# Chunked attention into a top-2 expert layer: x turned for the logits by transposing transfers instead of TensorE, and the turned P copied by ScalarE

## The chip, the cores and the metric

The kernel runs on one core of a Trainium2 chip. The metric is the device time of one execution in microseconds, the median of several runs. The engines are TensorE (PE, with PEld for its weight loads), VectorE (DVE), ScalarE (ACT), GpSimd (POOL) and SyncE (SP); SPq and POOLq are the queues in which SP and POOL issue transfers (DMAs). Each engine works through its own instructions in order; semaphores make them wait for each other. SBUF is the memory on the core with 128 partitions, PSUM the one that TensorE writes.

## What is computed

An attention over chunks, whose output is the token matrix x of a mixture-of-experts layer:

```python
batch, n_heads, seq, head_dim = (4, 8, 768, 64)
chunk, left_ctx, right_ctx = (32, 16, 8)          # and 8 memory keys and values
for c in range(seq // chunk):
    k_full = np.concatenate([mem_k, k[:, :, l_start:r_end]], axis=2)
    v_full = np.concatenate([mem_v, v[:, :, l_start:r_end]], axis=2)
    scores = scale * np.matmul(q_c, k_full.transpose(0, 1, 3, 2))
    a = softmax(scores)
    out[:, :, c_start:c_end] = np.matmul(a, v_full)
x = out.transpose(0, 2, 1, 3).reshape(3072, 512)

logits = x @ w_gate
noisy_logits = logits + np.log1p(np.exp(x @ w_noise)) * noise
top2 = np.argpartition(-noisy_logits, 2, axis=1)[:, :2]     # 8 experts
# softmax over the two; then for each expert e and its tokens:
out[mask] += top2_w * (np.maximum(x[mask] @ w1[e], 0.0) @ w2[e])
```

## The kernel before, in words

The program has two stages. The attention stage makes x and the routing; the expert stage gathers the tokens of each pair of experts and runs the two expert matmuls. Here only the first matters.

The attention is worked in 16 pairs, n = 0 to 15, four to a batch (HP = 4). A loop over i runs the pairs as a pipeline: iteration i does the max and the exponential of pair i, the PV matmuls of pair i - 1, the scores of pair i + 1 and the turning of q and k of pair i + 2. For a pair n these steps exist, each named in the code:

- `qkT_pe` turns q and k on PE into PSUM; ACT copies them to SBUF (qT at L268, and kd in two halves at L276).
- `scores_pe` writes the scores ps_s (there is one such buffer, so the scores of pair i + 1 wait until the subtraction of pair i has read the last ones).
- `max_dve` (mx, L313) and `sub_dve` (sd, L318) are DVE's; ACT makes P = exp(sd) at L320.
- `PT_pe` turns P on PE into p_p (L327); `PT_dve` copies it to PT in SBUF (L332).
- `PV_pe` multiplies with the memory values (L341) and the values (L345) into ps_o.
- `mult_dve` divides (rec at L357, xrow at L358): xrow is the buffer of x of one batch, three of them in turn.
- `xT_pe` turns 6 blocks of 128x128 of xrow on PE into p_x (L369), and ACT copies them into xt (L371). xt has five buffers, one per pair.

After four pairs, `begin_route(b)` runs in iteration i = 4b + 6: `logits_pe(b)` multiplies the four xt tiles of batch b with the router weights wgn (24 matmuls at L380), and the steps s1 to s8 of `route(b)` are spread over the next iterations as "early" and "late" steps. Step s4 makes the gates (L463 to L466, into xrow) and issues the write of the batch's x rows to memory (`write_rows`, x_rows at L548), from which the expert stage gathers by index. After the loop comes the routing of batch 3.

The order of instructions on each engine is that of the code, written out by hand; nothing reorders it. SP's queue carries, besides the x_rows writes, the loads of the memory values (mv_nat), of the router weights (wgn_f, two loads, at i = 3) and of the noise (nz_all, four loads: one with wgn_f, one at the routing of batch 0, two at that of batch 1). The loads of q, k, v and the expert weights are issued by POOL. PSUM tiles of the kinds p_t, p_p, p_x and the routing's share three buffers (psT).

Of the kernel before, what the change touches and what calls it, by code (L numbers as in the profile page):

```python
# [13 lines left out]
BF16 = mybir.dt.bfloat16  # L14
# [10 lines left out]
def kernel(  # L25
# [14 lines left out]
    nc = tc.nc  # L40
    B, H, S, D = q.shape
# [11 lines left out]
    HP = H // 2  # L53
# [45 lines left out]
    def body():  # L99
        actx = ExitStack()  # L100
        ap_ = actx.enter_context(tc.tile_pool(name="ap", bufs=2))
# [14 lines left out]
        def new_group(g):  # L116
            qg = ap_.tile([128, 2 * GP, SJ * D], BF16, name="qg", bufs=3)
            kg = ap_.tile([128, 2 * GP, SJ * D], BF16, name="kg", bufs=3)
            groups[g] = (qg, kg, vbufs[turn_of[g]])
# [8 lines left out]
        def load_v(g):  # L128
            vg = groups[g][2]
            for hd in range(2 * GP):  # L130
                p0, gh = QW * hd, 2 * GP * g + hd

                def piece(c, n, j=0, nj=WP):
                    nc.gpsimd.dma_start(  # L134
                        out=vg[p0 + j:p0 + j + nj, c:c + n, hd, :, :].rearrange("p c e d -> p c (e d)"),
                        in_=bass.AP(v.tensor, v.offset + (gh * S + c * chunk + 2 * j - left_ctx) * D, [[2 * D, nj], [chunk * D, n], [1, 2 * D]]))

                first, last = gh == 0, gh == B * H - 1
                if first:
                    piece(0, 1, left_ctx // 2, WP - left_ctx // 2)  # L140
                if last:
                    piece(ncnk - 1, 1, 0, WP - right_ctx // 2)
                piece(int(first), ncnk - first - last)

        def zero_k(x):
            for hh in range(2):
                nc.vector.memset(kbufs[x][64 * hh:64 * hh + 64, 1 - hh, :], 0.0)

        def zero_v(x, j, eng=None):
            (eng or nc.vector).memset(vbufs[x][:, 6 * j:6 * j + 6], 0.0)  # L150
# [12 lines left out]
        for hd in range(2 * GP):  # L163
            nc.sync.dma_start(
                out=mv_nat[QW * hd + WP:QW * hd + QW].rearrange("p g e d -> p g (e d)"),
                in_=bass.AP(mem_v.tensor, mem_v.offset + hd * n_mem * D, [[2 * D, n_mem // 2], [2 * GP * n_mem * D, NG], [1, 2 * D]]))
# [88 lines left out]
        st = [dict() for _ in range(NPAIR)]  # L255
        xrows = {}

        def qkT_pe(n):
            g, i = divmod(n, GP)
            qg, kg, _ = groups[g]  # L260
            for nm, src in (("qT", qg), ("kT", kg)):
                p_t = psT.tile([128, SJ, 128], BF16, name="p_t", tag="tr")
                for j in range(SJ):
                    for hh in range(2):
                        nc.tensor.transpose(out=p_t[64 * hh:64 * hh + 64, j, :], in_=src[:, 2 * i + hh, j * D:(j + 1) * D], identity=identb)  # L265
                if nm == "qT":
                    st[n][nm] = ap_.tile([128, S], BF16, name=nm, bufs=4)
                    nc.scalar.copy(st[n][nm].rearrange("d (p j) -> d p j", j=SJ), p_t.rearrange("d j p -> d p j"))  # L268
                else:
                    st[n]["p_k"] = p_t  # L270
# [7 lines left out]
        UB = BT // 2  # L278
# [32 lines left out]
        def max_dve(n):  # L311
            mx = ap_.tile([128, 2, BT], F32, name="mx")
            nc.vector.tensor_reduce(out=mx, in_=st[n]["ps"], axis=AX, op=Alu.max)  # L313
            st[n]["mx"] = mx

        def sub_dve(n):
            sd = ap_.tile([128, 2, BT, CTX], F32, name="sd")
            nc.vector.tensor_tensor(out=sd, in0=st[n]["ps"], in1=bc4(st[n]["mx"], CTX), op=Alu.subtract)  # L318
            P = ap_.tile([128, 2 * UB, 4, QW], BF16, name="P")
            nc.scalar.activation(out=P.rearrange("p x h c -> p h x c"), in_=sd.rearrange("p x (h u) (e c) -> p (x h) (u e) c", h=2, e=2), func=Act.Exp, scale=scale)  # L320
            st[n]["P"] = P

        def PT_pe(n):
            P = st[n]["P"]
            p_p = psT.tile([128, 2 * UB, 128], BF16, name="p_p", tag="tr")
            for x in range(2 * UB):
                nc.tensor.transpose(out=p_p[:, x, :], in_=P[:, x, :, :], identity=identb)  # L327
            st[n]["p_p"] = p_p

        def PT_dve(n):  # L330
            PT = ap_.tile([128, 2 * UB, 128], BF16, name="PT")
            nc.vector.tensor_copy(PT, st[n]["p_p"])  # L332
            st[n]["PT"] = PT

        def PV_pe(n):
# [27 lines left out]
        def xT_pe(n):  # L363
            b, r = divmod(n, HP)
            y, half = divmod(r, 2)
            p_x = psT.tile([128, UB, 2, 128], BF16, name="p_x", tag="tr")
            for u in range(UB):
                for s in range(2):
                    nc.tensor.transpose(out=p_x[:, u, s, :], in_=xrows[b][:, UB * half + u, 128 * y + 64 * s:128 * y + 64 * s + 64].bitcast(BF16), identity=identb)  # L369
            xt = ap_.tile([128, UB, 2, 128], BF16, name="xt", bufs=5)  # L370
            nc.scalar.copy(xt, p_x)  # L371
            st[n]["xt"] = xt
# [180 lines left out]
        def begin_route(b):  # L553
            logits_pe(b)
            begin, *rest = route(b)
            begin()
            while pending:
                early_steps()
                late_steps()
            pending.extend(rest)  # L560
            for x in ((1,), (2, 3))[b] if b < 2 else ():
                load_noise(x)

        def early_steps():
            if pending:
                for fn in pending[0][0]:
                    fn()
# [19 lines left out]
        def ahead(i):  # L587
            return [i + 2] if i < NEAR else [n for n in (i + 2, i + 3) if n < NPAIR and (i == NEAR or n > i + 2)]

        NEAR = 5  # L590
        for i in range(NPAIR):
            if i >= 1:
                PT_pe(i - 1)
            max_dve(i)
            for n in ahead(i):
                qkT_pe(n)
            fresh = i >= 3 and (i - 3) % HP == HP - 1
            if fresh:
                begin_route((i - 3) // HP)
            early_steps()  # L600
            if i >= 1:
                PT_dve(i - 1)
            sub_dve(i)
            if i == 0:
                zero_v(1, 1)
                load_v(1)
                new_group(3)
                load_qk(3)
            if i == 1:
                zero_k(3)  # L610
            for n in ahead(i):
                kT_act(n)
            if i >= 1:
                PV_pe(i - 1)
            if i + 1 < NPAIR:
                scores_pe(i + 1)
            if i < NPAIR - 1:
                late_steps()
            if i in (2, 3, 4):
                zero_v(2, i - 2)  # L620
            if i >= 1:
                mult_dve(i - 1)
                if i - 1 == NPAIR - 2:
                    write_rows(B, B - 1, 0, UB, 0, XC)
            if i >= 2:
                xT_pe(i - 2)
            if i == 2:
                load_v(2)
                memory_values(2, NG)
            for n in ahead(i):  # L630
                g = n // GP + 3
                if n % GP == 1 and g < NG:
                    new_group(g)
                    load_qk(g)
            if i == 3:
                zero_v(2, 3, nc.gpsimd)
                ramps()
                load_router()
            if i == 4:
                load_v(3)  # L640
            if i == 5:
                constants()
            if i >= 4 and i % GP == 0 and i // GP + 2 < NG:
                load_v(i // GP + 2)
            if i == GP * (NG - 3) + 1:
                load_w1(0)
                load_w2(0)
                load_w1(1)
        n = NPAIR - 1
# [227 lines left out]
        for e in range(E):  # L877
# [38 lines left out]
            if e == E - 1:  # L916
# [3 lines left out]
                    out=out_part[NB], out_offset=bass.IndirectOffsetOnAxis(ap=s_si[:, 0:1], axis=0),  # L920
                    in_=spart[:, 0, :], in_offset=None, bounds_check=N - 1, oob_is_err=False)
# [6 lines left out]
    with tc.manual_schedule():  # L928
        kept = body()
# [3 lines left out]
    with tc.For_i(SPILL, end, 128) as i:  # L933
# [7 lines left out]
        for t in range(NP):  # L941
# [11 lines left out]
            out=xl, out_offset=None, in_=xd, in_offset=bass.IndirectOffsetOnAxis(ap=gi[:, 0:1], axis=0),  # L953
# [4 lines left out]
        xt = ld.tile([128, KP, CAP], BF16, name="xtl", bufs=1)  # L958
# [5 lines left out]
        with tc.For_i(0, E, 1) as e:  # L964
# [17 lines left out]
            out=out, out_offset=bass.IndirectOffsetOnAxis(ap=si[:, 0:1], axis=0),  # L982
            in_=o, in_offset=None, bounds_check=N - 1, oob_is_err=False)
# [30 lines left out]
```

## Time and profile before

| | |
|---|---|
| median of 3 runs | 334.02 us (332.93 to 334.89) |
| the profiled execution, its own time | 335.33 us |
| its span in the trace | 333.7 us |
| PE busy over the span | 288.1 us (86%) |
| DVE, ACT, POOL busy | 169.9, 133.4, 138.6 us |
| first max of the attention loop | 14.74 us |
| first gather of the expert stage | 114.24 us |
| mean granted TensorE clock | 0.957 of full speed |

The profile is of one execution. A row of a timeline or of the chain of waits begins with the start and the length in us; L with a number is the line of the code; `out<-in` are the tiles. A group of instructions has its count (x16), the busy time in us and the mean of one in ns, and behind the bar the idle time before them and what ended it. The chain of waits is followed back from the last instruction: at each step to what released it. "issue" is time in which an engine waited for nothing that the profile shows.

### The profile page before, as it was taken

The page shows a single profiled execution, that of the slowest core. Times are in us where ns is not written, and L with a number is a line of the kernel's source. Part 1 is how long each engine was busy: PE and PEld are TensorE (multiplying, and loading weights), DVE is VectorE, ACT ScalarE, POOL GpSimd, SP SyncE. Part 2 cuts the span into 40 slices and gives each one's busy share as a digit, 9 for nine tenths or more (in the row PEclk, how much of TensorE's full clock was granted, in tenths as well). Part 3 has the DMA queues.
Part 4 walks back from the last instruction along what each step waited for, and adds up shares of the span by engine and source line. Part 5 has one row for each costly group of instructions (what it writes and reads, how often), then busy time and mean ns, then how long its engine had stood idle before and what let it go on. Part 6 is the DMA issues. An engine that isn't in the chain of part 4 may idle for free.

```text
span 333.7 us, 7301 instructions
## 1 busy us (share of the span) xinstructions
PE 288.1 (86%) x3019; PEld 173.5 (52%) x3019; DVE 169.9 (51%) x343; ACT 133.4 (40%) x235; POOL 138.6 (42%) x181
## 2 busy tenths in 40 slices
PE   1697887977776377999999999999999999999990
PEld 0575675755654256554754754544544544544540
DVE  7789859849958775222322323424342433434451
ACT  7877788757433033533333332332303303202200
POOL 7877868538023472781008007007152042042152
PEclk9999999979989559999999999999999999999997
DMA  7999999999997136699407905914959624521031
GB/s 99 179 163 176 184 163 163 210 143 101 214 225 216 23 88 93 128 156 238 87 0 125 221 4 110 223 28 105 207 147 166 117 111 70 86 109 60 1 140 71
DMA packets 58763, 42.99 MB, mean 129 GB/s; under 512 B 32449, under 2 KB 52033, under 8 KB 58728
## 3 DMA queue, kind: packets, MB, share of 16 engines
q0 software_dynamic: 49808, 38.71, 77.0%
q1 hardware_dynamic: 8632, 3.74, 5.6%
q8 instruction: 24, 0.39, 0.5%
q10 hardware_dynamic: 288, 0.07, 0.1%
q14 instruction: 11, 0.09, 0.1%
HBM read 61.23 MB, written 10.66 MB: 215 GB/s over the span
## 4 chain that ended last, share of the span: by engine, by line
PE 43%; issue 24%; DVE 13%; ACT 8%; POOL 7%; DMA 3%; POOLq 0%; DVEq 0%; ACTq 0%
PE ps_h L769 16%; PE ps_y L780 14%; POOL out_dram L788 4%; ACT kd L276 3%; PE ps_o L345 3%; DMA out_dram<-acc,sidx 2%; PE ps_o L341 2%; DVE mx L313 2%; DVE xrow L358 2%; DVE sd L318 2%; DVE vg L150 2%; PE p_t L705 2%; ACT xt L371 1%; ACT P L320 1%; PE p_t L265 1%
## 5 line engine op out<-in xcount | busy, mean ns | idle before, releaser
L769 PE MATMUL ps_h<-xTb,w1t 128*128 128x512 bf16 (+5 forms) x640 | 101.4, 320 | 1.5 <-DVE xTb L706 1.5
L780 PE MATMUL ps_y<-w2t,ht 128*128 128x512 bf16 x448 | 101.4, 379 | 0.0
L769 PEld LDWEIGHTS <-w1t 128*128 128x128 bf16 x640 | 58.6, 99 | 43.9 <-DVE xTb L706 1.1
L788 POOL DMA_INDIRECT out_dram<-acc,sidx x28 | 28.1, 1004 | 126.4 <-DVE acc L787 124.1
L756 DVE TENSOR_SCALAR ht<-ps_h 128x512 bf16<-128x512 f32 (+3 forms) x68 | 38.1, 560 | 68.1 <-PE ps_h L769 63.1
L780 PEld LDWEIGHTS <-ht 128*128 128x128 bf16 x448 | 42.9, 98 | 46.7
L754 ACT ACTIVATE ht<-ps_h 128x384 bf16<-128x384 f32 (+2 forms) x76 | 38.9, 511 | 70.4 <-PE ps_h L769 66.3
L784 ACT ACTIVATE acc<-ps_y,meta 128x512 f32<-128x512 f32 x28 | 19.2, 687 | 62.6 <-PE ps_y L780 45.4
L787 DVE SCALAR_TENSOR_TENSOR acc<-ps_y,meta,acc 128x512 f32<-128x512 f32 x28 | 21.0, 750 | 34.5 <-PE ps_y L780 34.5
L696 POOL DMA_INDIRECT xl<-x_rows,gidx x28 | 30.0, 1071 | 16.8 <-PE ps_h L769 6.6
L134 POOL DMA_DIRECT2D vg<-in_v_dram x34 | 25.5, 756 | 11.4 <-DMA kg<-in_k_dram 3.7
L706 DVE COPY xTb<-p_t 128x512 bf16<-128x512 bf16 x28 | 11.6, 422 | 28.6 <-PE p_t L705 28.4
L276 ACT COPY kd<-p_t 64x768 bf16<-64x768 bf16 x32 | 25.2, 786 | 1.0 <-PE p_t L265 0.8
L265 PE MATMUL p_t<-identb,qg 128*64 128x128 bf16 x192 | 10.3, 245 | 12.0 <-DMA qg<-in_q_dram 6.6
L371 ACT COPY xt<-p_x 128x768 bf16<-128x768 bf16 x16 | 12.8, 798 | 12.0 <-PE p_x L369 11.9
L341 PE MATMUL ps_o<-memv,PT 128*128 128x260 bf16 x96 | 15.0, 296 | 2.2 <-DVE PT L332 2.0
L320 ACT ACTIVATE P<-sd 128x768 bf16<-128x768 f32 x16 | 13.5, 845 | 8.1 <-DVE sd L318 8.1
L268 ACT COPY qT<-p_t 128x768 bf16<-128x768 bf16 x16 | 12.8, 800 | 8.9 <-PE p_t L265 8.8
L358 DVE TENSOR_TENSOR xrow<-ps_o,rec 128x768 bf16<-128x768 f32 x16 | 15.3, 958 | 0.6
L313 DVE TENSOR_REDUCE mx<-ps_s 128x12 f32<-128x768 f32 x16 | 15.1, 942 | 0.5 <-PE ps_s L300 0.5
L318 DVE TENSOR_TENSOR sd<-ps_s,mx 128x768 f32<-128x768 f32 x16 | 15.2, 949 | 0.0
L345 PE MATMUL ps_o<-vg,PT 128*32 128x256 bf16 x384 | 14.9, 293 | 0.0
(150 smaller groups left out, 287.5 us busy)
## 6 DMA issues: line engine op xcount, KB each, us to landing
w1t<-in_moe_w_dram POOLq DMA_DIRECT2D x8, 1024.0 KB, 11.4
w2t<-in_moe_w_dram POOLq DMA_DIRECT2D x8, 1024.0 KB, 10.1
vg<-in_v_dram POOLq DMA_DIRECT2D x30, 168.0 KB, 10.2
qg<-in_q_dram POOLq DMA_DIRECT2D x7, 384.0 KB, 9.9
kg<-in_k_dram POOLq DMA_DIRECT2D x7, 384.0 KB, 11.3
x_rows<-xrow SPq DMA_DIRECT2D x3, 792.0 KB
x_rows<-xrow SPq DMA_DIRECT2D x2, 384.0 KB
xl<-x_rows,gidx POOLq DMA_INDIRECT x28, 6.5
```

Of the source, the lines that this page charges most:

```text
L134: nc.gpsimd.dma_start(out=vg[p0 + j:p0 + j + nj, c:c + n, hd, :, :].rearrange("p c e d -> p c (e d)"), in_=bass.AP(v.tensor, v.offset + (g ...
L276: nc.scalar.copy(st[n]["kT"][hs, hh, :].rearrange("d (p j) -> d p j", j=SJ), st[n]["p_k"][hs].rearrange("d j p -> d p j"))
L313: nc.vector.tensor_reduce(out=mx, in_=st[n]["ps"], axis=AX, op=Alu.max)
L318: nc.vector.tensor_tensor(out=sd, in0=st[n]["ps"], in1=bc4(st[n]["mx"], CTX), op=Alu.subtract)
L345: nc.tensor.matmul(out=po[32 * r:32 * r + 32, u, :MD], lhsT=PT[:, 2 * u + e, 32 * r:32 * r + 32], rhs=vg[:, CB * half + x, :, e, :], start ...
L358: nc.vector.tensor_tensor(out=xr.rearrange("p u (h d) -> p u h d", d=D), in0=po[:, :, :MD].rearrange("p u (h d) -> p u h d", d=D), in1=rec ...
L696: nc.gpsimd.indirect_dma_start(out=xl, out_offset=None, in_=xd, in_offset=bass.IndirectOffsetOnAxis(ap=idx[:, p:p + 1], axis=0), bounds_ch ...
L754: nc.scalar.activation(out=dst, in_=src, func=Act.Relu)
L756: nc.vector.tensor_scalar(out=dst, in0=src, scalar1=0.0, scalar2=None, op0=Alu.max)
L769: nc.tensor.matmul(out=ps_h[:, o:o + w], lhsT=w1t[:, kp, f * 128:(f + 1) * 128], rhs=rhs(kp), start=(kp == 0 and i == 0), stop=(kp == KP - ...
L780: nc.tensor.matmul(out=ps_y, lhsT=ht[:, f, j * CAP:(j + 1) * CAP], rhs=w2t[:, f, :], start=(f == 0), stop=(f == FB - 1))
L788: nc.gpsimd.indirect_dma_start(out=out_part[p], out_offset=bass.IndirectOffsetOnAxis(ap=sidx[:, p:p + 1], axis=0), in_=a, in_offset=None, ...
```

## The change

For the batches 0 to 2 (pairs 0 to 11) the six blocks of a pair's x are no longer turned on PE and copied by ACT: SP issues six transposing transfers of 128x128 bf16 each (32 KB), from xrow straight into xt. That is 72 transfers, and 72 PE transposes and 12 ACT copies fewer. Batch 3 is turned as before. For the same twelve pairs the copy of the turned P (PT) is made by ACT and not by DVE, and it stands in the code right behind PE's turning of P, ahead of the turning of q and k, instead of behind the early steps.

```diff
         def PT_dve(n):
             PT = ap_.tile([128, 2 * UB, 128], BF16, name="PT")
-            nc.vector.tensor_copy(PT, st[n]["p_p"])
+            (nc.scalar.copy if n < HP * (B - 1) else nc.vector.tensor_copy)(PT, st[n]["p_p"])
             st[n]["PT"] = PT
...
         def xT_pe(n):
             b, r = divmod(n, HP)
             y, half = divmod(r, 2)
+            if b < B - 1:
+                xt = ap_.tile([128, UB, 2, 128], BF16, name="xt", bufs=5)
+                for u in range(UB):
+                    for s in range(2):
+                        nc.sync.dma_start_transpose(out=xt[:, u, s, :], in_=xrows[b][:, UB * half + u, 128 * y + 64 * s:128 * y + 64 * s + 64].bitcast(BF16))
+                st[n]["xt"] = xt
+                return
             p_x = psT.tile([128, UB, 2, 128], BF16, name="p_x", tag="tr")
...
         for i in range(NPAIR):
             if i >= 1:
                 PT_pe(i - 1)
+                if i - 1 < HP * (B - 1):
+                    PT_dve(i - 1)
             max_dve(i)
...
             early_steps()
-            if i >= 1:
+            if i - 1 >= HP * (B - 1):
                 PT_dve(i - 1)
             sub_dve(i)
```

SP's queue up to the end of the attention stage, before:

```order
L164 DMA mv_nat<-in_mem_v_dram 4x8x128 x4
L209 DMA wgn_f<-in_moe_w_gate_dram 128x4x8
L209 DMA wgn_f<-in_moe_w_noise_dram 128x4x8
L215 DMA nz_all<-in_moe_noise_dram 128x6x8 x2
L548 DMA x_rows<-xrow 128x6x264
L215 DMA nz_all<-in_moe_noise_dram 128x6x8 x2
L548 DMA x_rows<-xrow 128x6x264
```

The same queue after the change, up to the same place:

```order
L164 DMA mv_nat<-in_mem_v_dram 4x8x128 x4
L370 DMA_TRANSPOSE xt<-xrow 128x128 x12
L209 DMA wgn_f<-in_moe_w_gate_dram 128x4x8
L209 DMA wgn_f<-in_moe_w_noise_dram 128x4x8
L215 DMA nz_all<-in_moe_noise_dram 128x6x8
L370 DMA_TRANSPOSE xt<-xrow 128x128 x12
L215 DMA nz_all<-in_moe_noise_dram 128x6x8
L370 DMA_TRANSPOSE xt<-xrow 128x128 x12
L555 DMA x_rows<-xrow 128x6x264
L370 DMA_TRANSPOSE xt<-xrow 128x128 x12
L215 DMA nz_all<-in_moe_noise_dram 128x6x8 x2
L370 DMA_TRANSPOSE xt<-xrow 128x128 x12
```

Twelve transposes are those of two pairs. Those of pairs 0 and 1 now stand ahead of the router weights; those of pairs 6 and 7 stand behind the x_rows write of batch 0; behind the last row shown come the x_rows write of batch 1 and then the twelve of pairs 10 and 11.

ACT around the first routing (iterations 5 and 6) as a piece of the difference; the routing's lines have moved by seven (L395 is now L402):

```order
 L276 COPY kd_88<-p_t 64x768 x2
 L276 COPY kd_85<-p_t 64x768 x2
-L371 COPY xt<-p_x 128x768
+L332 COPY PT<-p_p 128x768
 L268 COPY qT<-p_t 128x768
-L395 ACTIVATE ns<-ps_l 128x48
-L396 ACTIVATE ns<-ns 128x48
-L399 COPY lg<-ps_l 128x48
+L402 ACTIVATE ns<-ps_l 128x48
+L403 ACTIVATE ns<-ns 128x48
+L406 COPY lg<-ps_l 128x48
 L320 ACTIVATE P<-sd 128x4x6x32
```

The PT copy of pair 5 stands where the xt copy of pair 3 stood, between kd and qT.

## The prediction, made before the change was run

> **What bounds the kernel now.** I read four views in this order: the page, the chain of waits from 14 us to 115 us, the timelines of VectorE (DVE) and of SyncE's queue (SPq), and the DMA view. From about 130 us on, the expert matmuls keep TensorE (PE) busy and the change touches nothing there. What it touches is the attention stage, whose end passes straight on. These are rows of the chain (start in us, length in us, what):
>
> ```profile
> 24.60 0.32 issue
> ...
> 47.27 0.74 PE ps_l L380 x24
> ...
> 56.68 0.32 issue
> ...
> 62.68 0.47 DVE PT L332
> ...
> 70.01 0.74 PE ps_l L380 x24
> ...
> 74.06 0.44 PE p_x L369 x6
> ...
> 89.62 0.36 PE p_x L369 x6
> 90.01 0.81 ACT xt L371
> 90.86 0.74 PE ps_l L380 x24
> ...
> 105.39 0.41 PE ps_l L380 x10
> ```
>
> The logits matmuls (L380) of batches 0 to 2 start at 47.27, 70.01 and 90.86 us, and the last ten of batch 3 at 105.39; all four groups lie on the chain, which leads from the last of them over the routing to the first gather and the first expert matmul. So a logits group that starts late pushes everything behind it, one for one.
>
> Between them the pairs run every 4 to 6 us, and no engine bounds all of them: the chain changes between DVE, ScalarE (ACT) and PE. The other pieces quoted are those where the edited steps show. "issue" of 0.32 us stands there four times between the max (mx) and the subtraction (sd) of a pair; the first is at 24.60 and the last at 56.68. It is a busy DVE, as its own timeline shows: the copy of the turned P (L332) runs in that gap.
>
> ```profile
> 22.72 0.96 DVE L358 TENSOR_TENSOR xrow<-ps_o,rec 128x768 bf16<-128x768 f32 x1
> 23.59 0.95 DVE L313 TENSOR_REDUCE mx<-ps_s 128x12 f32<-128x768 f32 x1
> 24.46 0.55 DVE L332 COPY PT<-p_p 128x768 bf16<-128x768 bf16 x1
> ```
>
> **What is removed and swapped.** The groups by line, with count, busy us and mean ns:
>
> ```profile
> L332 DVE COPY PT<-p_p 128x768 bf16<-128x768 bf16 x16 | 8.8, 550 | 0.8 <-PE p_p L327 0.6
> L371 ACT COPY xt<-p_x 128x768 bf16<-128x768 bf16 x16 | 12.8, 798 | 12.0 <-PE p_x L369 11.9
> L268 ACT COPY qT<-p_t 128x768 bf16<-128x768 bf16 x16 | 12.8, 800 | 8.9 <-PE p_t L265 8.8
> ```
>
> Twelve of the 16 copies of PT leave DVE: 12 x 0.55 = 6.6 us, which is the upper bound of what DVE can give back. On the chain they appear as four pieces of 0.32 us and one of 0.47 us, 1.75 us together. On ACT, twelve xt copies of 0.798 us go and twelve PT copies of the same shape come; a PSUM copy of that shape into another tile (qT) takes 0.800 us, so ACT's load is unchanged: 0 us. The PT copy now stands ahead of the qT copy instead of xt, in the place xt had, so nothing on ACT is later; its cover is that exchange, and without it (ACT holding PT back behind the two kd copies) it would cost up to 0.80 us a pair. On PE, 72 transposes go; the chain holds 0.44 + 0.36 us of them, and the xt copy ahead of the third logits is 0.81 us: 1.6 us. **The gain is 1.75 + 1.6 = 3.4 us**, between 0 (if each freed piece uncovers another engine) and 6.6.
>
> **What is added: 72 transposing transfers on one queue.** The trace has no such transfer. These are the nearest rows: SPq's timeline, the tile nz_all (durations min/median/max in ns), and the queue of SyncE's transfers.
>
> ```profile
> 2.18 1.39 SPq L164 DMA_DIRECT2D mv_nat<-in_mem_v_dram  x4
> 3.62 0.41 SPq L209 DMA_DIRECT2D wgn_f<-in_moe_w_gate_dram  x1
> 6.03 0.39 SPq L209 DMA_DIRECT2D wgn_f<-in_moe_w_noise_dram  x1
> 6.46 2.47 SPq L215 DMA_DIRECT2D nz_all<-in_moe_noise_dram  x2
> 58.80 0.37 SPq L548 DMA_DIRECT2D x_rows<-xrow  x1
> 59.22 3.26 SPq L215 DMA_DIRECT2D nz_all<-in_moe_noise_dram  x2
> ```
>
> ```profile
> L215 SPq DMA_DIRECT2D nz_all<-in_moe_noise_dram x4: 665/1344/2292, 6.5 to 60.2; - x4
> ```
>
> ```profile
> q1 hardware_dynamic: 8632, 3.74, 5.6%
> ```
>
> Call T the time SPq needs per transposing transfer in a row of them. Below, T is the shortest plain issue there, 0.37 us for x_rows with 768 pieces. Above, it is set by pieces: q1's 8632 packets took 5.6% of 16 engines over the span of 333.7 us, 34.6 ns each, so a load cut as finely as nz_all (768 pieces of 32 B) takes 768 x 34.6 / 16 = 1.66 us; the four in the timeline held SPq 1.23 and 1.63 us each, so the price fits. A transposing transfer moves 32 KB against nz_all's 24 KB, from 128 rows into 128 others; into how many pieces it falls, no row says. Between 0.37 and 1.66 I take the middle, **T = 1.0 us**. The range keeps both ends, and beyond them the longest nz_all issue, 2.29 us.
>
> Then the landing time, L. The second wgn_f load waited for a mv_nat transfer, as the waits of SPq say:
>
> ```profile
> SPq L209 <- DMA mv_nat<-in_mem_v_dram: 2.0, 1, 2.0
> ```
>
> Issued between 2.18 and 3.57 us and landed by 6.03: 2.5 to 3.9 us. I take L = 3 us.
>
> The queue is in order, and the order after the change has two x_rows writes between the transposes: the write of batch 0 stands ahead of pairs 6 and 7, that of batch 1 ahead of pairs 10 and 11. Each waits for its batch's gates on DVE, which come after that batch's logits. The second one:
>
> ```profile
> 83.23 0.37 SPq L548 DMA_DIRECT2D x_rows<-xrow  x1
> ```
>
> So after 83.23 us the queue must still issue the twelve transposes of pairs 10 and 11 and land the last before 90.86 us. Through the queue step by step, with T = 1.0 and L = 3:
>
> Batch 0. The first transposes can start when pair 0's xrow is there, 22.72 + 0.96 = 23.68. Twelve: 35.7. The two wgn_f loads and one nz_all (0.41 + 0.39 + 1.23): 37.7. Twelve more: 49.7, landed 52.7. Wanted at 47.27: **5.4 us late**.
>
> The router weights wgn_f, loaded at 3.62 us before, now land at about 36.5 + 3 = 39.5. DVE casts them here:
>
> ```profile
> 45.91 0.19 DVE L242 CAST wgn<-wgn_f 128x64 bf16<-128x64 f32 x1
> ```
>
> That leaves 6.4 us to spare; only from T = 1.5 would this cast wait, and the max of pair 6 behind it on DVE.
>
> Batch 1. One nz_all, then twelve for pairs 4 and 5: 49.7 + 1.2 + 12 = 62.9. The x_rows write of batch 0 is due at 58.80 + 5.4 = 64.2 and holds the queue until 64.6. Twelve for pairs 6 and 7: 76.6, landed 79.6. Wanted at 70.01 + 5.4 = 75.4: **4.2 us late**, 9.6 in sum.
>
> Batch 2. Two nz_all (3.26), twelve for pairs 8 and 9: 91.8. The x_rows write of batch 1 is due at 83.23 + 9.6 = 92.8, done 93.2. Twelve: 105.2, landed 108.2. Wanted at 90.86 + 9.6 = 100.5: **7.7 us late**.
>
> Together 17.3 us. While PE waits at a logits group, behind it stand the PV matmuls of the pair and the next scores; DVE waits for both, and ACT for DVE. No engine works ahead far enough to save this.
>
> The sum on the profiled execution (span 333.7, its own time 335.33): 335.3 + 17.3 - 3.4 = 349.2. That execution lies 1.3 us above the median of the three runs, 334.02, so against the median I predict **348 us**.
>
> The Trainium skill ("VectorE: DVE Perf Modes", section on the three transpose paths) gives 1309 ns for a 128x128 bf16 transpose by DMA against 390 ns on TensorE. With T = 1.31 the same steps give 12.9 + 10.3 + 14.2 = 37.4 us late, 368 us against the median. No run here shows the first figure yet; for the second, TensorE's transposes here are shorter:
>
> ```profile
> L369 PE MATMUL p_x<-identb,xrow 128*128 128x128 bf16 x96 | 8.4, 226 | 0.2 <-DVE xrow L358 0.2
> ```
>
> **Rivals.** *The transfers are on time* (faster). At T = 0.37 the twelve after 83.6 us take 4.4 + 3 = 7.4 us, and 90.86 - 83.6 is 7.3: next to nothing is late, and the gain stands: 335.3 - 3.4 = 331.9, against the median 331. For it: the plain x_rows issue with 768 pieces also held SPq for only 0.37 us. Against it: nz_all with as many pieces held it three to four times as long, and six to twelve transfers stand here in a row. The same skill ("Advanced Engine Details and Errata", section X-Bar Transpose (TRN2)) says that transposing DMAs run as fast as regular ones; by that rule this rival is the case, and nothing here shows it.
>
> *Even.* Between them, about T = 0.64, only batch 2 is late, by 3.4 us, and eats the gain: 334.
>
> *The queue is far slower than its nearest row.* T = 1.66 gives 21.3 + 18.7 + 22.6 = 62.6 us late, 393 against the median; T = 2.29 gives 108 us late, 439. For it: the longest nz_all, and loads fill the DMA engines here. Against it: 2.29 is one of four.
>
> *The transfers are on time, but take the DMA engines from the loads* (slower). Between 20 and 92 us:
>
> ```profile
> DMA packets 31692, 12.27 MB, mean 170 GB/s; under 512 B 23757, under 2 KB 31167, under 8 KB 31679
> ...
> vg<-in_v_dram POOLq DMA_DIRECT2D x26, 168.0 KB, 10.3
> ```
>
> 72 x 32 KB = 2.36 MB more, 13.9 us at 170 GB/s. The last v loads are issued from 74.12 us and used at 97.57 us:
>
> ```profile
> 74.12 3.62 POOL L134 DMA_DIRECT2D vg<-in_v_dram  x5 [0.28 <-PE ps_s L305]
> ```
>
> ```profile
> 97.57 1.41 PE ps_o L345 x24
> ```
>
> Issued by 77.7 and landed 10.3 us later, at 88.0, they have 9.5 us to spare; 13.9 - 9.5 = 4.4 us late, less the gain: about 1 us slower at least, 335 to 336, and up to 12.6 us slower if the spare time is used up earlier: 339 on average of the two ends. It decides as soon as the loads' landing passes about 20 us.
>
> **How the numbers follow.** Chances: forecast (T from about 0.75 to 1.66, 336 to 393) 0.54; far slower queue 0.15; loads held up 0.05; even 0.09; on time 0.17. The forecast's own case alone spans 336 to 393; the on-time end is 331, so the range goes from 330 to 400, which leaves out most of the far slower queue and a gain above my 3.4 us. Half a per cent, 1.7 us, is what a measurement of this kernel can tell from no change. Slower by more: 0.54 + 0.15 + 0.05 = 0.74; same 0.09; faster 0.17.
>
> **What will show it.** In the profile after: the length and spacing of the transposes on SPq give T; under 0.5 us the forecast is wrong. The waits of PE must show L380 (its new number) waiting for a DMA into xt, three times, the third the longest. The x_rows writes of batches 0 and 1 must stand in SPq with transposes queued right behind them. DVE's group of PT copies falls to four, ACT's grows to twelve near 0.80 us. If the logits of batch 2 start near 87 us, the on-time rival is right; if PE or POOL wait for vg or kg instead, the loads are.

## The result, and the profile after

| | before | after |
|---|---|---|
| median, us | 334.05 (332.93 to 334.89, 4 runs) | 386.29 (385.83 to 389.89, 4 runs) |
| ratio to before | | 1.159, 95% interval 1.1512 to 1.1667 |
| profiled execution's own time, us | 335.33 | 385.83 |
| its span, us | 333.7 | 384.2 |

The change costs 52 us. The direction of the prediction held and the time lies inside its range, but the loss is nearly four times the one forecast.

**Where the time came in.** The first gather of the expert stage, before and after (engine POOL; start, length, line, output<-inputs):

```profile
114.24 1.19 POOL L696 DMA_INDIRECT xl<-x_rows,gidx  x1 [2.82 <-DVE ov L807]
```

```profile
165.20 1.19 POOL L705 DMA_INDIRECT xl<-x_rows,gidx  x1 [2.64 <-DVE ov L814]
```

It is 51.0 us late, and the span is 50.5 us longer. From the gather to the end it is 333.7 - 114.2 = 219.5 us before and 384.2 - 165.2 = 219.0 after: everything was lost in the attention stage.

**The transfers.** SyncE's queue after the change, as its timeline shows it (start and length in us of a row of transfers):

```profile
23.22 17.73 SPq L370 DMA_TRANSPOSE xt<-xrow  x12
40.99 0.59 SPq L209 DMA_DIRECT2D wgn_f<-in_moe_w_gate_dram  x1
...
44.21 20.87 SPq L370 DMA_TRANSPOSE xt<-xrow  x12
65.12 0.58 SPq L215 DMA_DIRECT2D nz_all<-in_moe_noise_dram  x1
65.80 16.80 SPq L370 DMA_TRANSPOSE xt<-xrow  x12
82.70 0.53 SPq L555 DMA_DIRECT2D x_rows<-xrow  x1
83.33 19.62 SPq L370 DMA_TRANSPOSE xt<-xrow  x12
...
104.27 16.10 SPq L370 DMA_TRANSPOSE xt<-xrow  x12
120.47 0.53 SPq L555 DMA_DIRECT2D x_rows<-xrow  x1
121.10 20.61 SPq L370 DMA_TRANSPOSE xt<-xrow  x12
```

The six rows of twelve add up to 111.7 us, 1.55 us a transfer. Each row begins where the one ahead of it ended, so from 23.2 to 141.7 us the queue goes from one transfer to the next. A row's length also holds waits between its transfers. The waits of SPq show the main ones (sum in us, times, longest):

```profile
SPq L370 <- DMA x_rows<-xrow: 2.8, 1, 2.8
...
SPq L370 <- DMA xt<-xrow: 2.3, 2, 1.6
SPq L370 <- DVE xrow L358: 1.6, 1, 1.6
```

That is 6.7 us. For 1.6 us, in the third row, the queue stood for the x of the next pair. For 5.1 us, in the last row, it stood until earlier transfers had landed: first the x_rows write of 120.47, then two transposing ones. So the transposing transfers themselves took 105 us, 1.46 us each. In the view of the tile xt (durations min/median/max in ns, start of the first and of the last) the median is well below that mean, and the longest is three times the median:

```profile
L370 SPq DMA_TRANSPOSE xt<-xrow x72: 1093/1232/3962, 23.2 to 140.5; - x72
```

The hardware queue's line of the page counts the pieces:

```profile
q1 hardware_dynamic: 20152, 6.11, 10.4%
```

That is 20152 - 8632 = 11520 packets more than before, 160 a transfer, and 10.4% x 16 x 384.2 - 5.6% x 16 x 333.7 = 340 us more of DMA-engine time: 340 / 72 / 16 = 0.30 us of all 16 engines for each transfer, if the pieces are spread evenly over the engines. That is a fifth of the 1.55 us, so the pieces do not look like what holds the queue; the experiments test it.

**Who waits.** The waits between 14 and 165 us (engine, what waited, on what: sum in us, times, longest):

```profile
ACT ns L402 <- PE ps_l L387: 56.1, 4, 22.3
PE ps_l L387 <- DMA xt<-xrow: 44.6, 25, 11.9
...
DVE wgn L242 <- DMA wgn_f<-in_moe_w_noise_dram: 1.5, 1, 1.5
```

TensorE stands 25 times at the logits (now L387) for a transfer into xt, 44.6 us in all, and ScalarE stands behind it. The chain of waits shows the end of each of the three groups (start, length, what):

```profile
63.84 6.75 DMA xt<-xrow
70.64 0.19 PE ps_l L387
...
101.71 2.39 DMA xt<-xrow
104.16 0.19 PE ps_l L387
...
122.30 15.75 DMA xt<-xrow
138.07 1.09 SPq L370
...
140.48 2.33 DMA xt<-xrow
142.86 0.19 PE ps_l L387
```

The transfer issued at 122.30 us is one of those for which the queue itself stood: it landed at 138.05, and only then came the next one, at 138.07. Before, the three groups ended at 47.27 + 0.74 = 48.01, 70.75 and 91.60 us. Now the first ends at 70.64 + 0.19 = 70.83, the others at 104.35 and 143.05:

| end of the logits, us | before | after | added lateness | predicted |
|---|---|---|---|---|
| batch 0 | 48.01 | 70.83 | 22.8 | 5.4 |
| batch 1 | 70.75 | 104.35 | 10.8 | 4.2 |
| batch 2 | 91.60 | 143.05 | 17.8 | 7.7 |
| sum | | | 51.4 | 17.3 |

The 51.4 us account for the whole loss. The copies of PT did move as announced (count, then busy us and mean ns of one, then idle time ahead):

```profile
L332 ACT COPY PT<-p_p 128x768 bf16<-128x768 bf16 x12 | 9.6, 798 | 10.6 <-PE p_p L327 10.4
L332 DVE COPY PT<-p_p 128x768 bf16<-128x768 bf16 x4 | 2.2, 548 | 0.0
```

### The profile page after: what moved, and what is told of

Read it like the earlier page. It is cut to its first block, busy times and chain, and to the rows that moved or that the text cites. A ratio compares the mean times of both kernels' runs of the same rounds, so it can differ in the third digit from the quotient of the medians.

```text
span 384.2 us, 7262 instructions
## 1 busy us (share of the span) xinstructions
PE 294.2 (77%) x2947; PEld 175.0 (46%) x2947; DVE 164.9 (43%) x331; ACT 132.7 (35%) x235; POOL 138.5 (36%) x181
## 3 DMA queue, kind: packets, MB, share of 16 engines
q1 hardware_dynamic: 20152, 6.11, 10.4%
## 4 chain that ended last, share of the span: by engine, by line
PE 33%; issue 20%; SPq 15%; DVE 12%; DMA 10%; POOL 6%; ACT 2%; POOLq 0%; DVEq 0%
SPq L370 14%; PE ps_h L778 14%; PE ps_y L789 13%; DMA xt<-xrow 7%; POOL out_dram L797 4%; DMA out_dram<-acc,sidx 2%; DVE xrow L358 2%; PE ps_o L345 2%; DVE mx L313 2%; PE ps_o L341 2%; DVE vg L150 1%; PE p_t L714 1%; DVE sd L318 1%; ACT kd L276 1%; POOL xl L705 1%
## 5 line engine op out<-in xcount | busy, mean ns | idle before, releaser
L387 PE MATMUL ps_l<-wgn,xt 128*128 128x16 bf16 x96 | 9.1, 181 | 45.6 <-DMA xt<-xrow 44.6
L357 DVE RECIPROCAL rec<-ps_o 128x12 f32<-128x12 f32 x16 | 3.6, 223 | 69.4 <-PE ps_o L345 69.3
L387 PEld LDWEIGHTS <-xt 128*128 128x128 bf16 x96 | 5.7, 103 | 49.1 <-DMA xt<-xrow 47.1
L414 POOL TENSOR_TENSOR nl<-ns,nz_all 128x48 f32<-128x48 f32 x3 | 0.9, 287 | 61.3 <-ACT lg L406 61.3
L345 PE MATMUL ps_o<-vg,PT 128*32 128x256 bf16 x384 | 17.4, 328 | 4.1 <-DMA vg<-in_v_dram 4.1
L402 ACT ACTIVATE ns<-ps_l 128x48 f32<-128x48 f32 x4 | 0.8, 210 | 56.1 <-PE ps_l L387 56.1
L341 PE MATMUL ps_o<-memv,PT 128*128 128x260 bf16 x96 | 16.7, 318 | 3.9 <-DVE PT L332 2.9
L320 ACT ACTIVATE P<-sd 128x768 bf16<-128x768 f32 x16 | 13.5, 845 | 6.9 <-DVE sd L318 6.7
## 6 DMA issues: line engine op xcount, KB each, us to landing
w2t<-in_moe_w_dram POOLq DMA_DIRECT2D x8, 1024.0 KB, 10.4
vg<-in_v_dram POOLq DMA_DIRECT2D x30, 168.0 KB, 10.7
```

What stands on the lines that cost most here:

```text
L341: nc.tensor.matmul(out=po[:, u, :OW], lhsT=PT[:, 2 * u + e, :], rhs=memv[:, g, e, :], start=(e == 0), stop=False, skip_group_check=True)
L345: nc.tensor.matmul(out=po[32 * r:32 * r + 32, u, :MD], lhsT=PT[:, 2 * u + e, 32 * r:32 * r + 32], rhs=vg[:, CB * half + x, :, e, :], start ...
```

## The experiments

Three theories stood against each other. The first: SP's queue pays a fixed price per transposing instruction, whatever it moves. The second: the price follows the bytes or the pieces. The third: the transfers and the loads that run beside them (q, k, v, then the expert weights) hold each other up. The expectations refer to the theories by name or by letter: the first is A, the second B, the third C. D, in the runs with transfers for which nobody waits, says that the turning holds up the loads, and not the traffic as such. What each theory would give stands beside it.

The runs were made in four series, each on one chip together with runs of the kernel before (the expectations say call for series). Each ratio is against those; it is estimated from the single runs and can differ a little from the quotient of the medians. The medians of before lay between 333.88 and 338.77 us in the four series, so absolute times of different series are not compared. The difference lies behind the attention stage: from the first gather to the end the profiled executions took 219.0 to 219.5 us where before took about 334 us, and 224.1 to 225.4 us in the three other series, whatever the kernel. What makes this difference is not known. Nor does one profiled execution settle a few us: the same kernel (the plain copies below) had its first gather at 119.01 us in one series and at 115.41 in another.

### One half of the change at a time

Only the PT copies on ACT; x is turned by TensorE as before:

```diff
-            nc.vector.tensor_copy(PT, st[n]["p_p"])
+            (nc.scalar.copy if n < HP * (B - 1) else nc.vector.tensor_copy)(PT, st[n]["p_p"])
```

(and the place where PT_dve is called moved, as in the change.)

> Only the PT copies go to ACT; x is turned by PE as before. Theory A (the loss is all in the transposing transfers; the exchange of the PT copies is worth its pieces on the chain): 1.75 us off the four issue pieces and the one PT piece of the chain, less what ACT gives up with PT and xt both on it (0.80 us more a pair): between 329 and 334 us. Rival (the PT copy on ACT is itself a loss, since ACT now has both copies): 336 to 344 us.

Measured 338.23 against 337.88 us: 1.0016, interval 0.9981 to 1.005. No gain shows, and no loss: the time lies in the range of the rival only because before was slower in this series as well. The chain of this kernel has two pieces in the early pairs that the chain before did not have:

```profile
20.48 8.12 DMA vg<-in_v_dram
...
29.82 12.86 DMA vg<-in_v_dram
```

For 21 us the chain runs over the landing of v loads, so what DVE is spared there may end at a load. That is not shown: the control kernel further down leaves PT on DVE, takes as long as before, and has such pieces on its chain too (9.47 and 10.38 us for v, 11.02 us for k).

Only the transposing transfers; PT stays on DVE, at its old place:

```diff
-            (nc.scalar.copy if n < HP * (B - 1) else nc.vector.tensor_copy)(PT, st[n]["p_p"])
+            nc.vector.tensor_copy(PT, st[n]["p_p"])
```

> Only the transposing transfers; DVE copies PT as before. Theory A (SyncE's queue is the path, DVE's time is hidden behind it): 384 to 389 us, as the whole change. Rival (the PT copy on ACT causes part of the loss): clearly below the whole change, under 380 us.

Measured 391.72 against 337.88 us: 1.1608 (1.1536 to 1.1679), the whole loss. The rest of the study is about the transfers.

### The same bytes in half, and in twice, as many transfers

36 transfers of 128x256 (64 KB) instead of 72 of 128x128:

```diff
-                    for s in range(2):
-                        nc.sync.dma_start_transpose(out=xt[:, u, s, :], in_=xrows[b][:, UB * half + u, 128 * y + 64 * s:128 * y + 64 * s + 64].bitcast(BF16))
+                    nc.sync.dma_start_transpose(out=xt[:, u], in_=xrows[b][:, UB * half + u, 128 * y:128 * y + 128].bitcast(BF16))
```

> Each transposing transfer takes 128x256 in place of 128x128: 36 of 64 KB instead of 72 of 32 KB, the same bytes. Theory A (SyncE pays a fixed time for each instruction, 1.23 us, whatever its size): the queue needs 36 x 1.23 to 1.55 = 44 to 56 us instead of 112, the logits are late by some 2 to 8 us in all, and the time falls to 334 to 345 us. Rival B (the time goes by bytes, be it tiles or the crowded DMA engines): SPq holds 2.5 to 3.1 us per transfer, and the time stays at 380 to 390 us.

144 transfers of 64 rows (16 KB):

```diff
-                        nc.sync.dma_start_transpose(out=xt[:, u, s, :], in_=xrows[b][:, UB * half + u, 128 * y + 64 * s:128 * y + 64 * s + 64].bitcast(BF16))
+                        for z in (0, 64):
+                            nc.sync.dma_start_transpose(out=xt[:, u, s, z:z + 64], in_=xrows[b][z:z + 64, UB * half + u, 128 * y + 64 * s:128 * y + 64 * s + 64].bitcast(BF16))
```

> Each transposing transfer takes 64 rows by 128 columns: 144 of 16 KB, the same bytes. Theory A (fixed time per instruction): 144 x 1.23 = 177 us at least in the queue against 112, so 65 us or more on top: 445 to 500 us. Rival B (by bytes): 0.6 to 0.8 us each, 383 to 392 us.

Measured 373.14 us for the wide ones, 1.1044 (1.0984 to 1.1103), and 474.71 us for the half ones, 1.4078 (1.4002 to 1.4154), both against 337.88. The tile view of each (min/median/max in ns), the wide one first:

```profile
L369 SPq DMA_TRANSPOSE xt<-xrow x36: 1167/1320/4536, 23.2 to 113.6; - x36
```

```profile
L371 SPq DMA_TRANSPOSE xt<-xrow x144: 1132/1227/3495, 22.8 to 222.7; - x144
```

Medians of 1.32, 1.23 and 1.23 us for 64, 32 and 16 KB, which are 288, 160 and 96 packets by the counts on the three pages: a fourfold size changes the typical price by 8%. A stretch of the chain of the half-size kernel shows it undisturbed (from 62.99 to 89.68 us 22 transfers in a row read like these, one of them 1.17):

```profile
80.78 1.23 SPq L371
82.05 1.23 SPq L371
```

1.23 us and 0.04 us between them, 1.27 us each. That is the fixed price per instruction, as far as tried: all three sizes write into 128 partitions. The half-size kernel came out as the first theory had it. With half as many transfers it should then have left only 36 x 1.27 = 46 us on the queue, and the wide kernel should have come close to before. It came out between the times of the first two theories, 334 to 345 and 380 to 390 us, and neither had it right. The wide kernel's six rows on SP's queue, of which these are the first and the last,

```profile
23.23 8.88 SPq L369 DMA_TRANSPOSE xt<-xrow  x6
...
99.86 15.45 SPq L369 DMA_TRANSPOSE xt<-xrow  x6
```

add up to 76.6 us (with 12.15, 12.58, 12.69 and 14.83 between), 2.13 us a transfer. Part of that is the queue standing for its data, as the kernel's waits of SPq show:

```profile
SPq L369 <- DVE xrow L358: 10.3, 3, 4.1
```

Three times the queue had caught up and stood inside a row until the x of the next pair was made. What lies above 1.27 us a transfer and above such waits is 76.6 - 45.7 - 10.3 = 20.6 us there, 111.7 - 91.4 - 6.7 = 13.6 us in the change, and in the half-size kernel, whose six rows add up to 195.8 us, 195.8 - 182.9 = 13 us. So some transfers are slower than the fixed price, by 13 to 21 us in all, and wide ones most: 0.09, 0.19 and 0.57 us each on average for 16, 32 and 64 KB. The DMA engines' time per transfer rises as well: worked out as above (13.5% of 372.9 us on the wide kernel's page), it is 0.88 us of all 16 engines for a wide one against 0.30 us. So a price by pieces isn't the floor of 1.23 us, but it may be a part of what wide transfers pay above it. And the chain of the wide kernel leads over other transfers:

```profile
34.84 18.31 DMA kg<-in_k_dram
...
53.44 16.23 DMA vg<-in_v_dram
...
108.63 16.50 DMA xt<-xrow
```

k and v loads bound it early, and a transfer of its last row took 16.5 us to land, beside the expert weights.

### The weight loads out of the way

The loads of the expert weights are issued in iteration 15 of the loop over i instead of iteration 11, once with the change's transfers and once with the wide ones:

```diff
-            if i == GP * (NG - 3) + 1:
+            if i == NPAIR - 1:
                 load_w1(0)
```

> The change, with the first three expert weight loads issued in iteration 15 instead of 11, behind the third logits. Theory C (beside the fixed time per instruction, transposing transfers are held up by the big loads that share the DMA engines; the last twelve took 20.6 us in the queue and landed late while the weights were loading): the last twelve fall to 15 to 17 us and land in 2 to 3 us, 4 to 7 us off: ratio to before 1.139 to 1.150. Rival A alone (only the fixed time per instruction): the last twelve stay at 20 us and the ratio at 1.155 to 1.165.

> The wide transfers (36 of 128x256), with the weight loads in iteration 15. Theory C: the wait of 16.5 us for the last transfers falls to about 3 us, 10 to 14 us off the wide kernel: ratio 1.063 to 1.075. Rival (the wide transfers are slow by their bytes, whatever else is being loaded): the ratio stays at 1.10.

Measured 390.02 against 333.88 us, 1.1687 (1.1612 to 1.1761), and 360.18 us, 1.0764 (1.0696 to 1.0833). The first lies above both of its expectations, the second just above the range of the third theory. With the change's transfers, the last row of twelve fell from 20.61 to 15.93 us, and most of it now reads 1.22 to 1.23 us each on the chain:

```profile
128.33 1.23 SPq L370
129.60 1.23 SPq L370
...
137.25 2.34 DMA xt<-xrow
```

In the kernel with the transfers alone that row took 20.32 us too. The queue's waits for landings, 5.1 us of that row in the change, are gone. So the weight loads were what held up the last twelve, mainly by the late landing of earlier transfers. But the time was given back at once. The chain and the first gather of this kernel:

```profile
159.48 9.39 DMA x_rows<-xrow
```

```profile
169.77 1.19 POOL L705 DMA_INDIRECT xl<-x_rows,gidx  x1 [10.07 <-DMA x_rows<-xrow]
```

The last x_rows write now ran beside the moved weight loads, took 9.39 us to land, and POOL stood 10.07 us for it. With wide transfers the same wait stood there (9.39 us, the gather at 140.46 us), and still the ratio came down from 1.1044 to 1.0764.

### Transposes for which nobody waits

To see what the transfers do to the loads alone: the kernel before, with x turned by TensorE as it was, plus 24 wide transposing transfers of x of batches 0 and 1 into expert-weight tiles that are not yet in use. No instruction reads them. So that the queue ahead of the router's data is as short as before, the router weights and the noise are loaded at pair 1.

```diff
             st[n]["xt"] = xt
+            if b < 2:
+                for u in range(UB):
+                    z = UB * n + u
+                    dz = (w2bufs[0] if z < 16 else w1bufs[1]).rearrange("p a b -> p (a b)")[:, 256 * (z % 16):256 * (z % 16) + 256].rearrange("p (s c) -> p s c", c=128)
+                    nc.sync.dma_start_transpose(out=dz, in_=xrows[b][:, UB * half + u, 128 * y:128 * y + 128].bitcast(BF16))
```

> The kernel before, x turned by PE, and beside it 24 wide transposing transfers of the x of batches 0 and 1 into tiles that nobody reads until the weights come; the router weights and the noise are loaded early, so that nothing waits in the queue behind them. Theory C in its strong form (transposing transfers also hold up the q, k and v loads, which the pairs then wait for): 3 to 15 us slower, with landings of q, k and v above 10 us and PE or POOL waiting for them. Rival (the whole loss is the wait for x itself): within 0.5% of before.

Then the same with plain copies of the same bytes to the same places, and a control without any (the early loads alone):

```diff
-                    nc.sync.dma_start_transpose(out=dz, in_=xrows[b][:, UB * half + u, 128 * y:128 * y + 128].bitcast(BF16))
+                    nc.sync.dma_start(out=dz.rearrange("p s c -> p (s c)"), in_=xrows[b][:, UB * half + u, 128 * y:128 * y + 128].bitcast(BF16))
```

> As the idle transposes, but the 24 transfers are plain copies of the same 64 KB into the same places, untransposed. Theory D (the transposing itself, not the traffic, holds up the q, k and v loads): the copies cost SyncE 0.4 us each, the loads land in 10 to 11 us, and the time is within 1% of the control: ratio 0.995 to 1.01. Rival (it is the 1.5 MB of extra traffic on crowded DMA engines, turned or not): as slow as the idle transposes, ratio 1.03 to 1.05.

> The idle transposes taken out again; only the early loads of the router weights and the noise stay. Both theories: within 0.7% of before.

The transposes and the plain copies came from different series, so both ran once more in one:

> The kernel of e7 once more, now beside e12 against the same runs of the kernel before, since the medians of before differed by 1.5% between the calls of e7 and e9. Theory 'the turning itself holds the loads up': ratio about 1.043 again, and e12 about 3% below it. Rival 'the difference between e7 and e9 came from the two calls': e11 and e12 within 1% of each other.

> The kernel of e9 once more (plain copies of the same bytes in place of the 24 transposing transfers). Theory 'the turning itself': about 1.013. Rival 'any 64 KB copies within SBUF beside the loads do it': as e11, about 1.03 to 1.04.

| | this, us | before, us | ratio |
|---|---|---|---|
| 24 transposes | 348.22 | 333.88 | 1.0427 (1.0365 to 1.0488) |
| 24 plain copies | 343.26 | 338.77 | 1.0134 (1.0094 to 1.0174) |
| neither | 339.27 | 338.77 | 1.0008 (0.9963 to 1.0052) |
| 24 transposes, again | 353.48 | 338.42 | 1.0461 (1.0392 to 1.053) |
| 24 plain copies, same series | 341.68 | 338.42 | 1.011 (1.0046 to 1.0174) |

Copies of 24 x 64 KB within SBUF cost about 1% beside the loads, and turning them on the way costs a further 3%, though nobody waits for either. TensorE's granted clock differs too: between 40 and 65 us it was 0.73 of full speed with the transposes and 1.00 with the plain copies of the last two runs (0.80 and 0.86 in the first two). No run separates what the waits cost from what the lower clock costs. How long SP's queue is held, in the tile views of the last two (sixteen of the 24 go into w2t):

```profile
L378 SPq DMA_TRANSPOSE w2t<-xrow x16: 1170/1268/2826, 23.5 to 59.7; - x16
```

```profile
L378 SPq DMA_DIRECT2D w2t<-xrow x16: 465/600/1562, 23.7 to 53.2; - x16
```

1268 ns against 600 ns for the same bytes. And the wait of POOL, which issues the loads, for earlier v loads in the same two kernels, the transposing one first:

```profile
POOL vg L134 <- DMA vg<-in_v_dram: 11.5, 10, 3.2
```

```profile
POOL vg L134 <- DMA vg<-in_v_dram: 1.1, 2, 0.6
```

The landing itself is given for the first transposing kernel, and for the one before (DMA view from 20 to 80 us; the last column is the median us from issue to landing):

```profile
vg<-in_v_dram POOLq DMA_DIRECT2D x22, 168.0 KB, 17.3
qg<-in_q_dram POOLq DMA_DIRECT2D x5, 384.0 KB, 14.6
kg<-in_k_dram POOLq DMA_DIRECT2D x5, 384.0 KB, 16.1
```

```profile
qg<-in_q_dram POOLq DMA_DIRECT2D x5, 384.0 KB, 9.9
kg<-in_k_dram POOLq DMA_DIRECT2D x5, 384.0 KB, 11.3
```

q, k and v loads land in 14.6, 16.1 and 17.3 us instead of 9.9, 11.3 and 10.3 us (the last is the row for v that the prediction shows). The third theory is right about this: the transfers hold up the loads.

### Few enough to hide

Wide transfers for one pair in four only (the first of each batch, nine transfers in all, and its PT on ACT); the other pairs as before:

```diff
-            if b < B - 1:
+            if b < B - 1 and r == 0:
```

> Only the first pair of each of batches 0 to 2 is turned by wide transposing transfers (9 in all), and only its PT copy goes to ACT. The queue has three iterations to land each, so no logits wait. Theory C with little traffic, or A: 0.990 to 1.003 of before. Rival (any transposing transfer holds up the loads it meets): 1.005 to 1.02.

Measured 338.19 against 333.88 us: 1.0122 (1.0065 to 1.018), 1.2% slower. The waits of this kernel have none for xt, but the gather comes at 118.57 us, and one piece of the chain is this:

```profile
29.66 13.84 DMA vg<-in_v_dram
```

Nine transfers that are in time still cost more than is saved by the 18 turns on TensorE and the three copies that they replace. By what way is not shown: the loads landed only a little later (10.8, 12.0 and 10.7 us for q, k and v between 20 and 80 us), and the kernel with 24 plain copies has a like piece on its chain (14.34 us). No kernel of this study is faster than the one before.

## Why the prediction was wrong

**The failed step: the price of a transfer.** The prediction says: "Between 0.37 and 1.66 I take the middle, T = 1.0". T is 1.55 us. Its steps, worked again with 1.55 and otherwise the same numbers, give 18.6 + 16.1 + 20.0 = 54.7 us late where 51.4 were measured. By these steps the queue is through with the three groups at 62.9, 101.7 and 142.5 us; it was through at 65.1, 102.95 and 141.7. So the mechanism was right and the size of T was wrong, and the middle was no better than a guess. T is read from the run that it is checked against, and the groups one by one fit less well than their sum: 22.8, 10.8 and 17.8 us were measured. Both ends were built from the wrong quantity. A plain issue says what SP needs to start a plain transfer, and pieces say what the 16 DMA engines need. The price here is neither: 1.27 us per transposing instruction for 16 and 32 KB and hardly more for 64 KB, with the pieces of 32 KB needing about 0.30 us of 16 engines, plus 0.28 us on average, of which 0.19 us are slower transfers and 0.09 us waits of the queue. That the upper end by pieces, 1.66, comes near 1.55 is chance, since 288 pieces in one instruction instead of 160 cost 7% more in the median (1320 against 1232 ns).

The figure of the Trainium skill that the prediction set beside its own ("VectorE: DVE Perf Modes", section on the three transpose paths, 1309 ns by DMA) is near the measured floor of 1.23 to 1.32 us; with it the prediction would have been 368 us, short by what lies above the floor. The trace agrees with the figure to within some 6%, and the mean beside running loads is above it.

**What was right.** The three logits groups wait for xt; nothing behind them saves the time; the loss passes to the first gather one for one. The router weights came late as announced from T = 1.5 on: the cast waited 1.5 us.

**What was wrong in the steps, beside T.**
- *Lateness grows toward the third group.* It was largest at the first (22.8 us), where the first 24 transfers held the queue for 17.73 + 20.87 us against 12 + 12 predicted, and the last of them took 6.75 us to land where 3 were predicted.
- *The x_rows writes hold the queue.* At T = 1.55 they don't: the write at 82.70 starts where the transfers ahead of it end (65.80 + 16.80 = 82.60) and takes 0.53 us. The queue is so late by itself that the gates are done first. In the wide kernel the queue stood 3.7 us ahead of the first write and 2.8 us ahead of the second, so there the step works as described.
- *L = 3 us.* The last transfers of the groups took 6.75, 2.39 and 2.33 us, and one 15.75 us, beside the weight loads that start at about 114 us. The prediction had no step for those loads.
- *The gain of 3.4 us.* The half of it that lies with PT, 1.75 us, doesn't show: 1.0016 with an interval that reaches down to 0.9981, or 0.6 us. Where it went stays open: v loads stand on that kernel's chain, but loads stand on the control's as well. The other half, TensorE's and ACT's 1.6 us, could not be seen beside the waits, and the nine wide transfers show no such gain either.

**The rivals.** *On time* and *even* needed T up to 0.64 and fell with it. The rule of the Trainium skill behind the first ("Advanced Engine Details and Errata", section X-Bar Transpose (TRN2): as fast as regular DMAs) is not borne out for transfers of this size: 1268 ns of SP's queue against 600 for the same bytes, and 1.0461 against 1.011 in time. *A far slower queue*, at 1.66 us, gave 393 us and is the nearest of all in size. *The loads are held up* was priced by bytes and bandwidth (1 to 12.6 us), with the loads landing after 20 us as the point where it decides. The mechanism is real, at about 4% (14 to 15 us) with 24 wide transfers, and needs no 20 us; in the changed kernel TensorE waits 44.6 us for xt and 4.1 us for a v load, so most of it seems to lie hidden behind the queue.

**Open.** What makes up the 1.23 us of a transposing instruction, and by what way a transposing transfer holds up the loads of another queue, no run here shows. TensorE's granted clock also fell: from 14 us to the first gather it was 0.74 of full speed on average, against 0.93 before. What the lower clock adds behind each late group was not separated. Nor was it tried to issue the transfers from another queue.

## What to carry to other kernels

Price a new kind of transfer by a run of its own kind before moving work onto it: one issue can hold its queue for a time that follows neither its bytes nor its pieces, and then the count of instructions is what to cut (36 wide ones cost 10.4%, 72 cost 15.9%, 144 of half size cost 40.8%). Add up what an in-order queue must issue between the work's coming ready and its use: here 72 x 1.27 = 91 us of bare issue from 23.7 us on end at 115, and the third batch's logits were wanted at 90.86, in whatever order. And before a transfer replaces work of an engine that has slack, see whether the DMA engines are the ones without it: 24 wide transposing transfers for nobody cost 4%, and as plain copies 1%.

## What was not expected of the hardware

- A transposing transfer within SBUF holds SyncE's queue 1.23 us (0.04 us to the next), whether it carries 16 or 32 KB; at 64 KB the kernels with x turned this way had medians of 1.25 to 1.32 us.
- Beside loads some are slower (the longest of each kernel took 2.1 to 5.6 us), and they hold up the loads in turn: their landing went from 9.9 to 11.3 us to 14.6 to 17.3 us. Plain copies of the same bytes did much less of it (POOL waited 1.1 us for earlier v loads against 11.5 us).
- A plain x_rows write that met the 1 MB weight loads took 9.39 us to land, against 2.73 us in the kernel with nine transfers; a transposing transfer beside them took 15.75 us in one kernel and 16.50 us in another. In the first the queue stood 5.1 us for such landings.
